# Folding the odd channels with mirrored token blocks in a Fourier filter beside a gated feed-forward

## The chip, the cores and the metric

One core of one Trainium2 chip. The metric is the device time of one execution in microseconds; lower is better. A core has TensorE (matmuls, PE in the profile), VectorE (DVE), ScalarE (ACT), GpSimd (POOL) and SyncE (SP, which here only issues transfers), each with an instruction stream of its own, and 16 DMA engines that move data.

## The reference

`x` is 2048 tokens of 512 channels in bfloat16. It is normalized over its channels, goes through two branches, and the three are added:

```
xn = (x - mean(x)) / sqrt(var(x) + 1e-5)                 # per token
A  = irfft2( rfft2(xn) * (w_r + 1j*w_i) )                # over tokens and channels; w is 2048 x 257
B  = ( gelu(xn @ w_gate) * (xn @ w_up) ) @ w_down        # 512 -> 1792 -> 512
out = x + A + B
```

## The kernel before

**The gated branch.** The tokens stand in 16 blocks of 128, four blocks (512 tokens) to a group. For each group and each of 14 chunks of 128 hidden columns, `gated` runs four matmuls with `wg` and four with `wu` (line 686) over the turned tokens `xnT`; ScalarE takes gelu of the one (691) and a copy of the other (692) out of PSUM, and VectorE multiplies them into `hT` (693). `down` (731) then makes one block of 512 output channels out of 14 matmuls, and the result is added to `x_sb` (740, or 742 for the last group). The first two token blocks go through `first` (705) block by block, so that TensorE can begin before the other two are normalized.

**The Fourier branch.** Line by line:

- Each block is normalized into `xn` (a part of `specB`) and turned so that channels stand on partitions: the first four blocks by TensorE (`turn`, 554, and a copy by VectorE, 559), the other twelve by a transposing DMA (`turn_dma`, 563).
- `fold` (577 to 586) adds and subtracts the four channel quarters of a turned group. Even channel frequencies need quarter 0 + 2 and 1 + 3, added and subtracted once more, and are left with 128 rows each. Odd ones need 0 - 2 and 1 - 3: two sets of 128 rows. Then each block is added to, and subtracted from, its own token mirror image.
- The channel transform (597) has a folded token block as weights and the cosines and sines in `smallc` as the moving side. For one block it runs four matmuls: two of 128 columns for the even frequencies, and two of 256 columns for the odd ones, which accumulate the two sets. One tile holds two blocks; there are eight tiles, and ScalarE copies each out (602).
- VectorE folds the tokens in three butterfly stages (783 to 811); eight matmul tiles `v` with the table `tokf` (820, 823) finish the token transform.
- The product with the filter `filt` and its mirror image (849 to 880) is VectorE's, in two halves `B` of four tiles `v`. The filter's mirrored half stands in other rows of `w_r` and `w_i`, in reversed order. It is written reversed into a DRAM scratch tensor `w_mirror` (657 to 659) and loaded from there (662 to 666).
- The way back is the same in reverse: matmuls with `toki` (900, 901), butterflies (916 to 944), matmuls with `smallc` (960), the last folds (969 to 972), and the sum with `x_sb` (974).

So that mirror images of token blocks fit, the blocks before are shifted by 64 tokens: block n holds tokens 128n - 64 to 128n + 64, and the one that wraps around is loaded and stored in two halves (`halves`). `SL` gives the order of the blocks.

**The order of the work.** A planner (`_Sched.run`) simulates all engines with a cost for each operation and writes a fixed order for each engine; the chip then keeps that order and waits on semaphores. The operation that can start first is taken, and keys break ties. The gated and down matmuls carry the largest keys in the order in which they are written, so TensorE does them whenever nothing else is ready: they are the filler. An operation of TensorE that becomes ready late is planned a `MARGIN` of 1 us later still. Normalization and statistics of blocks 4 to 15 have due times (`NORM`, `STAT`).

**The first loads.** ScalarE issues the first third of `smallc` (the identity among it) and the first 384 columns of `wg` and `wu`. SyncE issues all other loads in the order of their keys: the first blocks of `x` one by one, columns 384 to 768 of the weights, `x` blocks 4 to 7, columns 768 to 1280 and 1280 to 1792, the rest of `smallc`, `x` blocks 8 to 15. The list `gate` holds back: from the third load on, everything on SyncE waits until the first block of `x` has landed, and the later tables wait for given normalizations. Eight warm-up matmuls on zeros (`warm`, 511) run before the data arrives, and two more between the first turns.

Of the kernel before, what the change touches and what calls it, by code (L numbers as in the profile page):

```python
# [12 lines left out]
S = 2048  # L13
D = 512
# [21 lines left out]

def _constants():
# [4 lines left out]
    K[0] = 8 * (2 * (m % 64) + m // 64)  # L42
    for v, c in enumerate((4, 1, 9, 2, 10, 3, 11)):
        K[v + 1] = c + 16 * m
# [4 lines left out]
    si2[:, 0, 0] = np.sin(th * q * 1024)  # L49
    cof = co.copy()  # L50
    cof[:, 0, 0] *= 0.5
    low = (m < 64)[None]
    tf = []
    for a in (cof, si2):
        for part in (low, ~low):
            e = a[:64, 0] * part
            tf.append(np.concatenate([e, 0 * e] if a is cof else [0 * e, e]))
    for v, c in enumerate((4, 1, 9, 2, 10, 3, 11)):
        g = -1.0 if c > 8 else 1.0
        c = min(c, 16 - c)  # L60
        if c % 2:
            r = np.sin(np.pi * c / 2)
            f = r * g, r
        else:
            f = (-1.0, 1.0) if c == 4 else (g, -1.0)
        tf.append(np.concatenate([co[:64, v + 1], f[0] * si[:64, v + 1]]))
        tf.append(np.concatenate([g * co[:64, v + 1], f[1] * si[:64, v + 1]]))
    tf = np.stack(tf, 1)
    ci, sv = co[:64].transpose(2, 1, 0), si2[:64].transpose(2, 1, 0)
    sg = np.array([0, 1, 1, 1, 1, -1, -1, -1])[:, None]  # L70
# [3 lines left out]
    for a in (pr, pi):  # L74
        half = a[:, 0, 0:64].copy()
        a[:, 0] = np.concatenate([half * lo, half * ~lo], 1)
# [25 lines left out]
class _V:  # L102


    def __init__(self, ap, buf, idx, cell, part=(0, 1)):
        self.ap, self.buf, self.idx, self.cell, self.part = ap, buf, idx, cell, part

    def __getitem__(self, sl):
# [3 lines left out]
        part = tuple(h for h in self.part if lo < 64 * (h + 1) and hi > 64 * h)  # L112
# [238 lines left out]
def bass_parallel_sum__spectral_gfnet__glu_gated_geglu__prompt_kernel(  # L351
# [15 lines left out]
    SL = (1, 2, 3, 0) + tuple(range(4, 16))  # L367
    xb = A_x[0][64:S - 64].rearrange("(a q) d -> q a d", q=P)

    def halves(t, n):  # L370
        return [(slice(0, P), t[0][P * n - 64:P * n + 64])] if n else [(slice(0, 64), t[0][S - 64:S]), (slice(64, P), t[0][0:64])]

# [7 lines left out]
    with ExitStack() as es:  # L380
# [22 lines left out]
        small = sb("smallc", [11, P])  # L403
# [23 lines left out]
        Tf = small[:, 1:7]  # L427
        Ti = small[:, 7:11]
# [46 lines left out]


# [7 lines left out]
        first_row = None  # L484
        for s in range(4):
            for part, rows in halves(A_x, SL[s]):
                o = load("sp", x[part, s], rows, 1024 * (part.stop - part.start), key=next(k))
            first_row = o if s == 0 else first_row
# [3 lines left out]
        wload("act", wg, wgv, 0, 384, key=0.5)  # L492
        wload("act", wu, wuv, 0, 384, key=0.5)
        for w, v in ((wg, wgv), (wu, wuv)):
            wload("sp", w, v, 384, 768, key=next(k))
        load("sp", x[:, 4:8], xb[:, 3:7, :], 524288, key=next(k))
        for lo, hi in ((768, 1280), (1280, FF)):
            for w, v in ((wg, wgv), (wu, wuv)):
                wload("sp", w, v, lo, hi, key=next(k))
        load("sp", small[:, 2:11].rs([9 * P]), c_small.ap()[:, 2 * P:], 294912, key=next(k))  # L500
        for b in (2, 3):
            load("sp", x[:, 4 * b:4 * b + 4], xb[:, 4 * b - 1:4 * b + 3, :], 524288, key=next(k))
        op("pool", 0.1, lambda e: e.memset(eps.ap, LN_EPS), writes=(eps,), key=-2)
        op("pool", 0.1, lambda e: e.memset(half.ap, -0.5), writes=(half,), key=0)
        op("dve", 0.2, lambda e: e.memset(zero.ap, 0.0), writes=(zero,), key=-90)


        wt = _T("dn")

# [502 lines left out]
```

## Time and profile before

| what | value |
|---|---|
| median of 3 runs | 174.16 us (173.99 to 174.22) |
| the profiled execution's own time | 173.99 us |
| its span, first to last instruction | 172.2 us |
| TensorE busy | 167.9 us (98%) |
| VectorE busy | 143.3 us (83%) |
| ScalarE busy | 106.2 us (62%) |
| GpSimd busy | 11.8 us (7%) |
| moved by DMA | 16.35 MB |

How to read it: a row of a group names the line, the engine, the operation, what it writes and reads, the shapes, how often (x), then the busy time in us and the mean of one in ns, and at last the idle time of the engine ahead of it with what ended that. Matmuls are pipelined and their ends are modelled, so the time of one is longer than the distance from one to the next. A line can be a helper's: 472 is every tensor-tensor operation of the Fourier branch, 468 every plain load. In the rows of transfers the number is the time from issue to landing. `SPq` and `ACTq` are the issuing of transfers. PEld is the loading of weights into TensorE.

### The profile page before, as it was taken

To read this page: it belongs to the slowest core of one execution; us is meant where nothing else is said; L and a number is where in the kernel's file an instruction comes from. 1 tells how busy PE (TensorE), PEld (TensorE's weight loads), DVE (VectorE), ACT (ScalarE), POOL (GpSimd) and SP (SyncE) were. 2 spreads that over 40 slices of the span, in tenths; PEclk is the share of its full clock that TensorE was granted. 3 is DMA by queue.
4 is the path that set the end of the run, shared out by engine and by line. 5 is a ranking of instruction groups with operands and counts; after the bars stand their busy time and mean duration, and the time that the engine had idled before them with its cause. 6 is when DMAs were issued, how large, how long until landed. Compare 5 with 4: busy or idle time off the path is not lost.

```text
span 172.2 us, 2683 instructions
## 1 busy us (share of the span) xinstructions
PE 167.9 (98%) x994; PEld 87.1 (51%) x994; DVE 143.3 (83%) x283; ACT 106.2 (62%) x172; POOL 11.8 (7%) x25
## 2 busy tenths in 40 slices
PE   7899999999999999999999999999999999999994
PEld 2588544455574444444444464554445664444443
DVE  2779899998539999967999999979999949972931
ACT  3378666675894647969645495794636996562000
POOL 2222234300000000030000000000000000000000
PEclk9999999999999999999999999999999999999999
DMA  5999999967532224920000000000000002410311
GB/s 150 299 356 354 298 145 300 231 151 144 122 81 63 61 52 97 308 71 4 0 2 0 0 4 0 0 0 0 4 0 2 0 4 81 129 36 0 122 64 61
DMA packets 24333, 16.35 MB, mean 95 GB/s; under 512 B 7679, under 2 KB 23936, under 8 KB 24320
## 3 DMA queue, kind: packets, MB, share of 16 engines
q1 hardware_dynamic: 23120, 15.32, 35.3%
q10 hardware_dynamic: 1200, 0.85, 1.6%
q8 instruction: 8, 0.13, 0.3%
q14 instruction: 5, 0.04, 0.1%
HBM read 12.50 MB, written 3.15 MB: 91 GB/s over the span
## 4 chain that ended last, share of the span: by engine, by line
PE 93%; DMA 4%; ACT 1%; DVE 1%; issue 0%; DVEq 0%
PE ps_gu L686 55%; PE ps_dn L731 21%; PE ps_sp L731 7%; DMA x_sb<-in_A_x_dram 4%; PE ps_sp L597 3%; PE ps_sp L960 2%; PE ps_sp L820 2%; PE ps_sp L900 1%; PE ps_sp L901 1%; ACT gg L716 1%; PE ps_sp L823 1%; DVE bst L524 0%; PE ps_gu L705 0%; PE ps_sp L554 0%; ACT uu L717 0%
## 5 line engine op out<-in xcount | busy, mean ns | idle before, releaser
L686 PE MATMUL ps_gu<-xnT,wu 128*128 128x512 bf16 (+1 forms) x236 | 56.7, 363 | 0.2 <-ACT gg L716 0.2
L686 PE MATMUL ps_gu<-xnT,wg 128*128 128x512 bf16 (+1 forms) x236 | 56.7, 363 | 0.0
L691 ACT ACTIVATE gg<-ps_gu 128x512 bf16<-128x512 f32 (+1 forms) x59 | 33.6, 570 | 13.1 <-PE ps_gu L686 10.4
L692 ACT ACTIVATE uu<-ps_gu 128x512 bf16<-128x512 f32 (+1 forms) x59 | 33.7, 572 | 10.8 <-PE ps_gu L686 10.5
L731 PE MATMUL ps_dn<-wd,hT 128*128 128x512 bf16 x168 | 38.9, 379 | 0.0
L686 PEld LDWEIGHTS ps_gu<-xnT,wg 128*128 128x128 bf16 x236 | 22.8, 98 | 22.9 <-DVE xnT L559 0.3
L686 PEld LDWEIGHTS ps_gu<-xnT,wu 128*128 128x128 bf16 x236 | 22.7, 98 | 22.9 <-ACT gg L716 0.4
L472 DVE TENSOR_TENSOR specB<-specB 128x1024 bf16<-128x1024 bf16 (+2 forms) x47 | 29.3, 662 | 1.5 <-ACT specB L965 1.4
L731 PEld LDWEIGHTS ps_dn<-wd,hT 128*128 128x128 bf16 x168 | 16.4, 98 | 19.1
L693 DVE TENSOR_TENSOR hT<-gg,uu 128x512 bf16<-128x512 bf16 (+1 forms) x59 | 22.5, 396 | 3.1 <-ACT uu L692 3.1
L739 ACT ACTIVATE db<-ps_dn 128x512 bf16<-128x512 f32 x12 | 7.2, 597 | 18.6 <-PE ps_dn L731 18.5
L524 DVE BATCH_NORM_STATS2 bst<-x_sb 128x6 f32<-128x512 bf16 x16 | 10.9, 685 | 3.6 <-DMA x_sb<-in_A_x_dram 3.6
L472 DVE TENSOR_TENSOR specC<-specB 128x1024 bf16<-128x1024 bf16 (+5 forms) x21 | 12.8, 634 | 0.2
L731 PE MATMUL ps_sp<-wd,hT 128*128 128x512 bf16 (+2 forms) x70 | 12.3, 336 | 0.0
L472 DVE TENSOR_TENSOR specB<-specA 128x2048 bf16<-128x2048 bf16 x8 | 9.4, 1220 | 2.9 <-ACT specA L602 2.4
L740 DVE TENSOR_TENSOR x_sb<-db,x_sb 128x512 bf16<-128x512 bf16 x12 | 5.0, 417 | 6.7 <-ACT db L739 6.7
L731 PEld LDWEIGHTS ps_sp<-wd,hT 128*128 128x128 bf16 x70 | 6.3, 97 | 6.1 <-DVE x_sb L742 0.2
L472 DVE TENSOR_TENSOR specB<-specB,filt 128x2048 bf16<-128x2048 bf16 x8 | 9.4, 1216 | 0.0
L828 ACT ACTIVATE specA<-ps_sp 128x1024 bf16<-128x1024 f32 x8 | 8.0, 1024 | 1.6 <-PE ps_sp L820 1.3
L602 ACT ACTIVATE specA<-ps_sp 128x1024 bf16<-128x1024 f32 x8 | 7.8, 1028 | 1.7 <-PE ps_sp L597 1.6
L965 ACT ACTIVATE specB<-ps_sp 128x1024 bf16<-128x1024 f32 x8 | 7.8, 1031 | 0.4 <-PE ps_sp L960 0.4
L906 ACT ACTIVATE specC<-ps_sp 128x1024 bf16<-128x1024 f32 x8 | 7.8, 1039 | 0.0
(64 smaller groups left out, 131.2 us busy)
## 6 DMA issues: line engine op xcount, KB each, us to landing
wd<-in_B_w_down_dram SPq DMA_DIRECT2D x1, 1792.0 KB, 8.8
out_dram<-x_sb SPq DMA_DIRECT2D x14, 128.0 KB, 1.8
x_sb<-in_A_x_dram SPq DMA_DIRECT2D x3, 512.0 KB, 8.8
wg<-in_B_w_gate_dram SPq DMA_DIRECT2D x2, 512.0 KB, 7.5
wu<-in_B_w_up_dram SPq DMA_DIRECT2D x2, 512.0 KB, 8.2
filt<-w_mirror SPq DMA_DIRECT2D x6, 128.5 KB, 5.2
toki<-c_ti SPq DMA_DIRECT2D x1, 768.0 KB, 7.9
tokf<-c_tf SPq DMA_DIRECT2D x1, 576.0 KB, 4.3
```

What stands on the lines that cost most here:

```text
L472: return op("dve", c_tt(n), lambda e: e.tensor_tensor(o.ap, a.ap, b.ap, f), reads=(a, b), writes=(o,), key=key, **kw)
L524: op("dve", 0.61, lambda e: e.bn_stats(bst[:, s].ap, xs(s).ap), reads=(xs(s),), writes=(bst[:, s],), key=key, due=due, after=after)
L602: op("act", c_act(1024), lambda e, yv=yv, t=t: e.activation(yv.ap, spair(t).rearrange("p (s r i) -> p s i r", s=4, r=4), ACT.Copy), writes ...
L686: ins = e.matmul(gub(t, n), w.ap[:, dc, fc * P:(fc + 1) * P], xnT.ap[:, b, sl, dc, :], start=(dc == 0), stop=(dc == 3))
L691: op("act", c_act(n), lambda e: e.activation(gg.ap[:, gs.slot, 0:n], gub(g, n), ACT.Gelu_apprx_tanh), tiles=(g, gs), key=0.0)
L692: op("act", c_act(n), lambda e: e.activation(uu.ap[:, us.slot, 0:n], gub(u, n), ACT.Copy), tiles=(u, us), key=0.0)
L693: op("dve", c_tt(n), lambda e: e.tensor_tensor(hT.ap[:, h.slot, lo:lo + n], gg.ap[:, gs.slot, 0:n], uu.ap[:, us.slot, 0:n], MUL), tiles=(g ...
L731: ins = e.matmul(bank(), hT.ap[:, hs[(b, fc)].slot, sl * P:(sl + 1) * P], wd.ap[:, fc, lo:lo + n], start=(fc == 0), stop=(fc == NFC - 1))
L739: op("act", c_act(n), lambda e: e.activation(db.ap[:, d.slot, 0:n], bank(), ACT.Copy), tiles=(t, d), key=0.0)
L828: op("act", c_act(1024), lambda e, xv=xv, t=t: e.activation(xv.ap, spair(t), ACT.Copy), writes=(xv,), tiles=(t,), key=-0.5)
L906: op("act", c_act(1024), lambda e, gv=gv, t=t: e.activation(gv.ap, spair(t).rearrange("p (k x i) -> p k x i", k=4, x=4), ACT.Copy), writes ...
L965: op("act", c_act(1024), lambda e, rv=rv, t=t: e.activation(rv.ap, spair(t), ACT.Copy), writes=(rv,), tiles=(t,), key=-0.5)
```

## The change

- The token blocks are the plain ones, tokens 128n to 128n + 127; `halves` and `SL` go, and each block is one load and one store.
- The odd channels are folded once more, as the even ones are. For that the second pair's difference is needed with its channels reversed: a new function `mirror` takes quarter 1 minus quarter 3 of the normalized block, read backwards along the channels, and turns it by itself, for the first group on TensorE and for the other three by a transposing DMA. `fold` then adds it to and subtracts it from quarter 0 minus quarter 2. The channel matrices shrink from six to four blocks of 128 columns, and the two matmuls of 256 columns become two of 128.
- The rows of the token tables (`tokf`, `toki`, the frequencies on partitions) run backwards in blocks of 32. With this the mirrored filter comes directly from `w_r` and `w_i`, and the near one is loaded reversed within blocks of 32; the DRAM scratch goes. The filter loads wait for the last mirrored difference. The rows for frequency zero move from partition 0 to partition 96.
- The last butterfly of the first token tile (a sum and a difference) goes into the table `tokf`.
- The order of the tiles `v` in the token transform and back changes, and the halves `B` take every second tile.
- The start: the first block is normalized, turned and copied in two halves (`first_half`); the reciprocal root for the second block is ScalarE's and VectorE's, not GpSimd's; the loads on SyncE wait, from the third on, for the third warm-up matmul and not for the first block; `x` blocks 8 to 11 go ahead of the last weight columns; the first token block's matmuls do all of `wg` ahead of `wu`, and the first of them waits for half of the channels.

The diff, cut to its core:

```diff
@@ the constants
-    for d0, r in ((0, (0,)), (0, (2,)), (0, (1, 3)), (P, (1, 3))):
-        kk = np.concatenate([np.arange(i, 256, 4) for i in r])[None]
-        ks = np.where(kk == 0, 256, kk)
-        a = 2.0 * np.pi / D * (d0 + np.arange(P) + 0.5)[:, None]
-        fwd += [np.cos(a * kk), np.sin(a * ks)]
+    a = 2.0 * np.pi / D * (np.arange(P) + 0.5)[:, None]
+    for r in (0, 2):
+        kk = np.arange(r, 256, 4)[None]
+        fwd += [np.cos(a * kk), np.sin(a * np.where(kk == 0, 256, kk))]
+    odd = np.concatenate([np.arange(1, 256, 4), np.arange(3, 256, 4)])[None]
+    fwd += [np.cos(a * odd), np.sin(a * odd)]
...
@@ the first loads
-            if s == 1:
-                gate.append(first_row)
...
+        rows(0, 1)
+        rows(1, 2)
+        gate.append(warms[2])
+        for i in (2, 3):
+            rows(i, i + 1)
         for w, v in ((wg, wgv), (wu, wuv)):
             wload("sp", w, v, 384, 768, key=next(k))
...
+        rows(4, 8)
+        for w, v in ((wg, wgv), (wu, wuv)):
+            wload("sp", w, v, 768, 1280, key=next(k))
+        rows(8, 12)
+        for w, v in ((wg, wgv), (wu, wuv)):
+            wload("sp", w, v, 1280, FF, key=next(k))
+        load("sp", small[:, 2:9].rs([7 * P]), c_small.ap()[:, 2 * P:], 229376, key=next(k))
+        rows(12, 16)
...
@@ the first block
+        def first_half(h):
+            cs = slice(2 * h, 2 * h + 2)
+            i, r, o = xs(0)[:, 256 * h:256 * h + 256], xn(0)[:, cs].rs([256]), xnT[:, 0, 0, cs].rs([256])
...
+            op("dve", 0.2, lambda e: e.tensor_scalar(r.ap, i.ap, bag.ap[:, 0, 0:1], rs.ap[:, 0:1], SUB, MUL), ...)
+            op("pe", 2 * 0.107, f, reads=(r, ident), tiles=(t,), key=-70.0, lag=0.1)
+            op("dve", 0.21, lambda e: e.tensor_copy(o.ap, bank()), writes=(o,), tiles=(t,), key=-70.0)
...
@@ the mirrored difference, and fold
+        def mirror(b):
+            rows = RB(8192 + 2048 * (b % 2), [4, 4, P])
+            g = RB(2048 * (b % 2) + 1024, [4, P])
+            odd[b] = RB(2048 * (b % 2) + 1536, [4, P])
+            tt(g, rows[:, :, 1, ::-1], rows[:, :, 3, ::-1], SUB, 512, 0.5)
+            if b:
+                op("sp", 1.25, lambda e: e.dma_start_transpose(odd[b].ap, g.rs([512]).ap), ..., dma=425000, key=-5.0)
+                return
...
+            op("pe", 4 * 0.056, f, reads=(g, ident), tiles=(t,), key=2.0, lag=0.1)
+            op("dve", 0.34, lambda e: e.tensor_copy(odd[b].rs([512]).ap, bank()), ..., key=1.0)
...
-            tt(f[:, :, 2:4], xt[:, :, 0:2], xt[:, :, 2:4], SUB, 1024, kk)
-            for i, n in ((0, 3), (3, 1)) if b == 0 else ((0, 4),):
...
+            tt(f[:, :, 3], xt[:, :, 0], xt[:, :, 2], SUB, 512, kk)
+            tt(f[:, :, 2], f[:, :, 3], odd[b], SUB, 512, kk)
+            tt(f[:, :, 3], f[:, :, 3], odd[b], ADD, 512, kk)
...
-                            to = bank[:, :, 2 * cc] if cc < 2 else bank[:, :, 1::2]
-                            mat = Tf.ap[:, cc] if cc < 2 else Tf.ap[:, 2 * cc - 2:2 * cc]
-                            ins = e.matmul(to, z.ap[:, p + o, cc, :], mat, start=(cc == 0), stop=(cc == 3))
+                            to = bank[:, :, 2 * cc] if cc < 2 else bank[:, cc - 2, 1::2]
+                            ins = e.matmul(to, z.ap[:, p + o, cc, :], Tf.ap[:, cc], start=(cc == 0), stop=(cc == 3))
...
@@ the filter
+        gate.append(hold[16])
         for ri, src in ((0, A_w_r), (1, A_w_i)):
...
+            near = src.rearrange("(a b c) k -> a b (c k)", a=4, b=32)[:, ::-1, 257:8 * 257]
+            far = src.rearrange("(a b c) k -> a b c k", a=4, b=32)
+            load("sp", W[:, ri, 0, 1:8], near, 460544, key=next(k), cost=0.55)
+            for h in range(4):
+                load("sp", W[32 * h:32 * h + 32, ri, 1, 1:8], far[3 - h, :, 15:8:-1], 115136, key=next(k), cost=0.55)
...
@@ the token transform
-        u = Fb[:, 2:4]
-        tt(u, s2[:, 0:2], s2[:, 2:4], ADD, 1024)
-        tt(H[:, 14], u[:, 0], u[:, 1], ADD, 512)
-        tt(H[:, 15], u[:, 0], u[:, 1], SUB, 512)
+        tt(H[:, 14:16], s2[:, 0:2], s2[:, 2:4], ADD, 1024)
...
-        for v, hh in enumerate(((14, 15), (12, 13), (0, 1), (4, 6), (8, 9), (10, 11), (2, 7), (5, 3))):
+        for v, hh in ((4, (12, 13)), (0, (14, 15)), (2, (8, 9)), (6, (10, 11)), (1, (0, 1)), (7, (4, 6)), (3, (2, 7)), (5, (5, 3))):
...
```

More of the change, by code (lines that the diff above doesn't have):

```diff
@@ L111, in __getitem__ @@
         lo, hi, _ = sl[0].indices(P)
-        part = tuple(h for h in self.part if lo < 64 * (h + 1) and hi > 64 * h)
+        part = tuple(h for h in self.part if lo < 32 * (h + 1) and hi > 32 * h)
         return _V(self.ap[sl], self.buf, self.idx[sl[1:]], self.cell, part)
@@ L474, in bass_parallel_sum__spectral_gfnet__glu_gated_geglu__prompt_kernel, with warm @@
         ADD, SUB, MUL = ALU.add, ALU.subtract, ALU.mult
+        op("dve", 0.2, lambda e: e.memset(zero.ap, 0.0), writes=(zero,), key=-90)
+        wt = _T("dn")
+        def warm(key):
+            return op("pe", 0.427, lambda e: e.matmul(ps_dn[:, :], zero.ap[:, 0:P], zero.ap, start=True, stop=True), reads=(zero,), tiles=(wt,), key=key)
+        warms = [warm(-50) for _ in range(WARM)]
         def load(q, dst, src, nbytes, **kw):
@@ L631, in bass_parallel_sum__spectral_gfnet__glu_gated_geglu__prompt_kernel @@
             if s % 4 == 3:
+                mirror(s // 4)
+                hold[16] = sch.ops[-2]
                 fold(s // 4)
```

190 lines of the change are left out of this document (88 added, 102 removed).

## The prediction

> **What bounds the kernel now.** I read the page first (busy times, the chain that ended last), then the waits of TensorE, then the chain in order of time.
>
> ```profile
> span 172.2 us, 2683 instructions
> ...
> PE 167.9 (98%) x994; PEld 87.1 (51%) x994; DVE 143.3 (83%) x283; ACT 106.2 (62%) x172; POOL 11.8 (7%) x25
> ...
> PE 93%; DMA 4%; ACT 1%; DVE 1%; issue 0%; DVEq 0%
> ```
>
> TensorE is busy 98% of the span, and 93% of the chain that ended last is its own work. Its waits (us in total, times, longest) are three:
>
> ```profile
> PE ps_dn L511 <- DVE zero L505: 1.2, 1, 1.2
> PE ps_gu L705 <- DVE xnT L559: 0.5, 1, 0.5
> PE ps_gu L686 <- ACT gg L716: 0.2, 1, 0.2
> ```
>
> L511 is the warm-up on zeros; the other two lie in the first 11 us, as the rows of part 2 show. So two things move the end: what is taken from or added to TensorE's work, and when its unbroken run begins. All else counts only where it makes TensorE wait. The chain (start us, us, what) gives the pieces:
>
> ```profile
> 11.55 0.45 PE ps_sp L554 x8
> ...
> 36.94 1.32 PE ps_sp L597 x16
> ...
> 133.06 0.89 PE ps_sp L960 x16
> ...
> 157.80 12.14 PE ps_sp L731 x70
> 169.96 0.29 DVE x_sb L742
> ```
>
> **Part 1: the channel matmuls (L597), on TensorE's path.** A tile of two token blocks has eight matmuls, four of 128 columns and four of 256; there are eight tiles (64 matmuls in all). Two tiles (x16) take 1.32 us, so 0.66 each. After the change all eight have 128 columns, since the odd channels come folded and there is no second half to accumulate. L960 has that very form, a token block as weights and 128 columns of smallc moving, and its x16 take 0.89 us: 0.445 a tile. Eight tiles save 8 x (0.66 - 0.445) = 1.72 us. The other end of the bound is that the weight loads set the pace, as there stays one for each matmul:
>
> ```profile
> L731 PEld LDWEIGHTS ps_dn<-wd,hT 128*128 128x128 bf16 x168 | 16.4, 98 | 19.1
> ```
>
> A load of 128 x 128 lasts 98 ns. Eight of them in series are 0.78 us a tile, 8 x 0.12 = 1.0 us more than now in all. I take 0.445, as the L960 row has one load to each matmul and still runs at 0.89 / 16 = 56 ns: the loads overlap. The Trainium skill (TensorE: Matmul & The Clock Gate, "Back-to-back issue gap") speaks against this change: it says that a stream of pairs of load and matmul sustains about 81 ns at 128 columns, and that 56 ns under-counts. By that a tile would be an estimated 0.65 us and the eight tiles would save 0.1 us. The L960 row, 56 ns in such a stream, disagrees.
>
> Block 0's mirrored half is turned on TensorE by four matmuls like those of L554, 0.45 / 8 x 4 = 0.23 us more. All other matmuls keep their number and shape: the token stage's first tile (four matmuls), the inverse stages, the gated and the down matmuls. Part 1: -1.72 + 0.23 = **-1.5 us**.
>
> **Part 2: the start.** Rows picked from the merged order of time (start us, us, engine, line):
>
> ```profile
> 1.17 4.45 PE L511 MATMUL ps_dn<-zero 128*128 128x512 bf16 x10 [1.17 <-DVE zero L505]
> ...
> 3.25 0.69 DVE L524 BATCH_NORM_STATS2 bst<-x_sb 128x6 f32<-128x512 bf16 x1 [2.14 <-DMA x_sb<-in_A_x_dram]
> ...
> 5.46 0.44 PE L554 MATMUL ps_sp<-smallc,specB 128*128 128x128 bf16 x4
> 5.50 0.51 SPq L468 DMA_DIRECT2D wu<-in_B_w_up_dram  x1
> ...
> 6.42 0.40 PE L705 MATMUL ps_gu<-xnT,wg 128*128 128x128 bf16 x4 [0.52 <-DVE xnT L559]
> ...
> 7.34 0.69 DVE L524 BATCH_NORM_STATS2 bst<-x_sb 128x6 f32<-128x512 bf16 x1 [0.65 <-DMA x_sb<-in_A_x_dram]
> ...
> 7.91 0.39 PE L705 MATMUL ps_dn<-xnT,wu 128*128 128x128 bf16 x4
> ...
> 8.42 0.40 PE L705 MATMUL ps_gu<-xnT,wg 128*128 128x128 bf16 x4
> ...
> 9.77 0.60 PE L686 MATMUL ps_gu<-xnT,wg 128*128 128x256 bf16 x4
> ...
> 10.52 0.60 PE L686 MATMUL ps_gu<-xnT,wu 128*128 128x256 bf16 x4 [0.15 <-ACT gg L716]
> ...
> 11.92 0.69 DVE L524 BATCH_NORM_STATS2 bst<-x_sb 128x6 f32<-128x512 bf16 x1 [0.33 <-DMA x_sb<-in_A_x_dram]
> ...
> 12.71 0.60 PE L686 MATMUL ps_gu<-xnT,wu 128*128 128x256 bf16 x4
> 13.32 0.61 PE L686 MATMUL ps_gu<-xnT,wg 128*128 128x256 bf16 x4
> ```
>
> At 56 ns a 128-column matmul and 112 ns a 256-column one (so a group issues in 0.23 or 0.45 us, shorter than the printed times, which hold the last one's end), TensorE's issue has four gaps: 5.69 to 6.42 (0.73), 8.14 to 8.42 (0.28), 10.22 to 10.52 (0.30), 13.16 to 13.32 (0.16). Together 1.47 us: the most that a better start can give.
>
> The first gap is the copy of the turned block 0, done in one piece. The change normalizes, turns and copies it in halves, and the first group's first two matmuls need only the first half. The warm-up (L511, ten at 0.44) still holds TensorE up to 5.46, so I put the first L705 near 6.0. The second gap: VectorE took the statistics of the third block of x ahead of the copy that TensorE needed, and waited until 7.34 for that block's load. The fourth is the same once more, behind statistics that waited until 11.92 for the next load. For the third, the transfers (KB, us to landing) say more than the releaser named:
>
> ```profile
> wu<-in_B_w_up_dram SPq DMA_DIRECT2D x1, 384.0 KB, 4.9
> ```
>
> wu's second piece, issued at 5.50, lands at 10.4, and TensorE goes on at 10.52. So three gaps of four hang on how early SyncE issues. Before, its third load waits until the first block of x has landed (3.25). After, it waits for the third warm-up matmul, 1.17 + 3 x 0.44 = 2.5, and one load less (the wrapped block's two halves) stands ahead of the weights. That is 0.75 us earlier, and for the weights up to 0.5 more (the issue at 5.50 lasts 0.51). The transfers can use only part of it, as the windows show (DMA share and GB/s last):
>
> ```profile
> 5.50:6.00 0.50, 0.40 (x5) 0.23 (x4) 0.06 (x1) 0.49 (x2) 0.42 (x1) 1.00 1.10 375
> 6.00:6.50 0.50, 0.07 (x2) 0.08 (x3) 0.50 (x2) 0.01 (x1) 0.16 (x1) 1.00 1.10 254
> 6.50:7.00 0.50, 0.50 (x8) 0.37 (x9) 0.19 (x1) 0.00 (x0) 0.00 (x0) 1.00 0.55 87
> 7.00:7.50 0.50, 0.50 (x13) 0.50 (x11) 0.16 (x1) 0.00 (x0) 0.00 (x0) 1.00 0.79 253
> ```
>
> From 6.0 to 7.5 the engines moved (121 + 288 + 122) x 0.5 = 266 KB less than at 375 GB/s, which is 0.7 us of transfer: the hole that the late issue left. Filling it brings every later load 0.7 us forward at most. Against it: the first pieces of wg and wu, issued by ScalarE, share the engines with what SyncE now issues sooner. I take 0.6 us of the 1.47; the bounds are +0.3 (wu's first piece pushed back by one x block, 128 KB at 375 GB/s) and -1.47. Part 2: **-0.6 us**.
>
> **Part 3: VectorE, off the path.**
>
> ```profile
> L472 DVE TENSOR_TENSOR specB<-specB 128x512 bf16<-128x512 bf16 x16 | 6.1, 416 | 0.0
> ...
> L472 DVE TENSOR_TENSOR specB<-xnT 128x1024 bf16<-128x1024 bf16 x8 | 5.2, 680 | 0.0
> ```
>
> Each block's fold loses one operation of 1024 and gains four of 512 (the mirrored difference, the first pair's difference, and their sum and difference): 4 x 0.416 - 0.68 = +1.0 us, +4.0 for four blocks. The token stage loses one of 1024 and two of 512 and gains one of 1024, -0.8. The copy of block 0's turned half is +0.4 and the joining of its two split folds about -0.3. Net +3.3 us, nothing on the path as long as gelu products and the spectral result come in time (rival B).
>
> **Part 4: the queue of SyncE.** Three more turns by DMA stand in it, each behind its block's other four, and the filter loads behind the last mirrored difference.
>
> ```profile
> L563 SPq DMA_TRANSPOSE xnT<-specB x12: 1188/1280/2376, 16.9 to 37.4; - x12
> ...
> DMA to landing us min/median/max: 3.2/4.2/7.1
> ...
> 38.73 4.36 SPq L468 DMA_DIRECT2D filt<-in_A_w_r_dram  x7
> ...
> 48.55 6.20 SPq L468 DMA_DIRECT2D w_mirror<-in_A_w_r_dram  x3
> ...
> 81.25 4.64 DVE L472 TENSOR_TENSOR specB<-specB,filt 128x2048 bf16<-128x2048 bf16 x4
> ```
>
> A turn is issued in 1.3 us and lands after 4.2, at worst 7.1. The filter is first read at 81.25. Reversing 1024 rows through DRAM took 6.2 us of issue, 6 ns a row; the direct loads move about 1300 rows for each part, so 2 x 7.8 us, and begun near 40 (the direct loads of before begin at 38.73, just behind the turns) they are issued by about 60. Cost nothing, with some 15 us in hand after a landing like that of a turn; without that cover VectorE would stall by what is lacking.
>
> **Sum.** On the profiled execution (173.99 us, of which 1.8 lie outside the span): -1.5 - 0.6 = -2.1, 171.9. The median of the runs shown is 174.16, 0.17 above it: **172.0 us**, likely 171.3 to 172.6.
>
> **Rivals.** A: the start gives nothing. wu's first piece lands later because x and the second pieces share the engines, and the gaps move but stay: 0 to +0.3 in place of -0.6, hence 172.6 to 173.0. For it: 375 GB/s at 5.5, no room there. Against it: the hole after 6.5.
>
> B, slower: the spectral result comes late to the last block. TensorE still has the last L731 run at 157.80, and VectorE must by then have added the spectral rows.
>
> ```profile
> 133.00:158.00 25.00, 25.00 (x165) 13.19 (x163) 19.06 (x35) 17.32 (x26) 0.00 (x0) 1.00 0.14 43
> ```
>
> VectorE (third busy time) has 5.9 us free there; TensorE's shorter run takes 1.5 of them. So a lateness above 4.4 us decides. VectorE's 3.3 us, and a last turn that lands in 7.1 rather than 4.2 (2.9) behind an issue of its own 1.3 us, make 7.5: 3.1 us too many, 175.1. Against it: the fold runs where VectorE has time between waits, and the early part of the spectral work has other slack. C: weight loads pace L597: +1.0 + 0.23 - 0.6, 174.8; at 81 ns a matmul -0.1 + 0.23 - 0.6, 173.7. Against it the L960 row. D: the planner's new order loses as much as the work saves (a wait of 2 us anywhere in TensorE's run): 174.1; nothing in the rows speaks for a place.
>
> **How the numbers follow.** Forecast 0.60; A 0.17; C at 81 ns 0.03, C at 98 ns 0.02; B 0.13; D 0.05. About 0.2% (0.35 us) is what this kernel's measurement can tell from no change. Faster is forecast, A and C at 81 ns: 0.80, less 0.02 for a start that loses more; same is D, 0.05; slower is B, C at 98 ns and that rest, 0.17. Range: from all four gaps closed (174.16 - 1.5 - 1.47 = 171.2, and 0.1 for the scatter of the runs: 171.1) up through A and C at 81 ns to D, 174.2.
>
> **What would show it.** Right: L597 has 64 matmuls of 128 columns at about 0.445 us a tile in the chain; TensorE's busy time falls by about the 1.5; the first L705 is near 6.0 and the wait before the first wu group of L686 is gone; VectorE busy near 146.6; no wait of TensorE after 14 us. Wrong: x16 of L597 above 1.2 us (C); a wait of L597 on specC, or of the last L731 on x_sb (B); the first L686 again near 9.8 and a hole in the DMA share (A).

## The result, and the profile after

The changed kernel takes 172.06 us (median of 4 runs, 171.99 to 172.15), the kernel before 174.07 us beside it (4 runs, 173.87 to 174.22). The ratio is 0.9885, with a 95% interval of 0.9868 to 0.9902: 1.7 to 2.3 us faster. The forecast was 172.0. The profiled execution after took 172.02 us, its span 170.0; the span is 2.2 us shorter.

First, from the page of the kernel after, the busy times and the chain by engine.

```profile
PE 166.2 (98%) x998; PEld 85.9 (51%) x998; DVE 146.1 (86%) x295; ACT 106.0 (62%) x173; POOL 11.5 (7%) x23
...
PE 95%; DMA 3%; DVE 1%; issue 0%; DVEq 0%
```

TensorE's busy time fell by 1.7 us, VectorE's rose by 2.8, and TensorE's share of the chain went from 93 to 95%. TensorE bounds the kernel as before, with less work. The waits of TensorE after (us in total, times, longest) are down to one, the warm-up on zeros:

```profile
PE ps_dn L476 <- DVE zero L470: 1.2, 1, 1.2
```

The two other waits of before, 0.5 and 0.2 us, are gone from this view, and there is none later than 14 us. The groups by form and the chain (start us, us, what) show the channel matmuls, which were L597 and are now L631:

```profile
L631 PE MATMUL ps_sp<-smallc,specC 128*128 128x128 bf16 x64 | 4.4, 219 | 0.0
...
42.03 0.89 PE ps_sp L631 x16
...
64.62 0.43 PE ps_sp L851 x2
...
98.29 0.06 PE ps_sp L931
...
130.83 0.89 PE ps_sp L991 x16
...
155.57 12.14 PE ps_sp L766 x70
```

All 64 have 128 columns now. Sixteen take 0.89 us where they took 1.32, which is 56 ns a matmul. (The 219 ns of the group is one matmul from start to end; the next is issued before that.) The same places in the chain of the kernel before that were not shown above:

```profile
61.24 0.43 PE ps_sp L820 x2
...
98.79 0.06 PE ps_sp L900
```

Read against each other, these rows tell where the spectral part ran late. The channel matmuls begin 5.1 us later than before (42.03 to 36.94), the token transform 3.4 later (64.62 to 61.24), the next spectral step 0.5 earlier (98.29 to 98.79), the inverse channel step 2.2 earlier (130.83 to 133.06), and the last run 2.2 earlier (155.57 to 157.80). The extra work on VectorE did delay the spectral part by several us, as rival B feared. By 98 us it had been made up with no wait of TensorE, since the gated matmuls filled its time.

The start, from the timeline of TensorE after (start us, us, engine, line):

```profile
5.44 0.54 PE L567 MATMUL ps_sp<-smallc,specB 128*128 128x128 bf16 x4
6.11 0.77 PE L737 MATMUL ps_gu<-xnT,wg 128*128 128x128 bf16 x8
...
7.61 0.39 PE L737 MATMUL ps_dn<-xnT,wu 128*128 128x128 bf16 x4
8.09 0.40 PE L737 MATMUL ps_gu<-xnT,wg 128*128 128x128 bf16 x4
...
9.44 0.60 PE L718 MATMUL ps_gu<-xnT,wg 128*128 128x256 bf16 x4
9.92 0.60 PE L718 MATMUL ps_gu<-xnT,wu 128*128 128x256 bf16 x4
10.43 0.61 PE L718 MATMUL ps_gu<-xnT,wg 128*128 128x256 bf16 x4
...
12.89 0.60 PE L718 MATMUL ps_gu<-xnT,wg 128*128 128x256 bf16 x4
```

With the issue times of the prediction (0.23 us for four matmuls of 128 columns, 0.45 for four of 256), the gaps are now 5.67 to 6.11 (0.44, was 0.73), 7.84 to 8.09 (0.25, was 0.28), 9.89 to 9.92 and 10.37 to 10.43 (0.09, was 0.30); the fourth (0.16) is gone. That is 0.78 us in place of 1.47. (The prediction's list left out a fifth gap: four matmuls issue in 0.23, and in before the next L705 after the one at 6.42 begins at 6.79, 0.14 too late. After has about as much between the halves, in the x8 row that lasts 0.77 where a later one of its form lasts 0.61, so the difference stands.) The seventh group of 256 columns begins at 12.89 rather than 13.32, although block 0's mirrored turn (four matmuls, 0.23) now stands ahead of it: 0.43 + 0.23 = 0.66 us won by the start. The sum closes: 1.72 - 0.23 + 0.66 = 2.15 against 2.2 in the span. It is a sum over one pair of profiles; the start scatters by several tenths, as said under Part 2.

### The profile page after: what moved, and what is told of

Its sections match the earlier page's. It is cut to its first block, busy times and chain, and to the rows that moved or that the text cites. A ratio compares the mean times of both kernels' runs of the same rounds, so it can differ in the third digit from the quotient of the medians.

```text
span 170.0 us, 2695 instructions
## 1 busy us (share of the span) xinstructions
PE 166.2 (98%) x998; PEld 85.9 (51%) x998; DVE 146.1 (86%) x295; ACT 106.0 (62%) x173; POOL 11.5 (7%) x23
## 4 chain that ended last, share of the span: by engine, by line
PE 95%; DMA 3%; DVE 1%; issue 0%; DVEq 0%
PE ps_gu L718 55%; PE ps_dn L766 21%; PE ps_sp L766 7%; DMA x_sb<-in_A_x_dram 3%; PE ps_sp L631 2%; PE ps_sp L991 2%; PE ps_sp L851 2%; PE ps_sp L931 1%; PE ps_sp L932 1%; PE ps_dn L476 1%; PE ps_gu L737 1%; PE ps_sp L854 1%; DVE bst L520 0%; PE ps_dn L737 0%; PE ps_sp L550 0%; DVE xnT L555 0%
## 5 line engine op out<-in xcount | busy, mean ns | idle before, releaser
L718 PE MATMUL ps_gu<-xnT,wg 128*128 128x512 bf16 (+1 forms) x236 | 56.7, 363 | 0.0
L718 PE MATMUL ps_gu<-xnT,wu 128*128 128x512 bf16 (+1 forms) x236 | 56.7, 363 | 0.0
L466 DVE TENSOR_TENSOR specB<-specB 128x512 bf16<-128x512 bf16 (+2 forms) x58 | 33.1, 609 | 3.8 <-DMA specB<-specB 2.3
L718 PEld LDWEIGHTS ps_gu<-xnT,wu 128*128 128x128 bf16 x236 | 22.8, 98 | 23.2
L718 PEld LDWEIGHTS ps_gu<-xnT,wg 128*128 128x128 bf16 x236 | 22.6, 98 | 22.3 <-ACT uu L752 0.2
L725 DVE TENSOR_TENSOR hT<-gg,uu 128x512 bf16<-128x512 bf16 (+1 forms) x59 | 22.6, 393 | 1.7 <-ACT uu L724 1.6
L466 DVE TENSOR_TENSOR specC<-specB 128x1024 bf16<-128x1024 bf16 (+2 forms) x18 | 12.4, 712 | 0.2
```

Source lines behind the costliest of these rows:

```text
L466: return op("dve", c_tt(n), lambda e: e.tensor_tensor(o.ap, a.ap, b.ap, f), reads=(a, b), writes=(o,), key=key, **kw)
L718: ins = e.matmul(gub(t, n), w.ap[:, dc, fc * P:(fc + 1) * P], xnT.ap[:, b, sl, dc, :], start=(dc == 0), stop=(dc == 3))
L725: op("dve", c_tt(n), lambda e: e.tensor_tensor(hT.ap[:, h.slot, lo:lo + n], gg.ap[:, gs.slot, 0:n], uu.ap[:, us.slot, 0:n], MUL), tiles=(g ...
```

## The experiments

Every kernel here was run beside the kernel before, so ratios are to that; after's is 0.9885. The planner writes each engine's order afresh for each kernel. b_gate keeps before's order on every engine, a_gate0 keeps after's, and a_ord0 keeps after's on all but SyncE. For the others the order moved elsewhere too, which is said where it matters.

### The shorter matmuls

a_rep: the changed kernel with the first quarter of each token block's contraction issued three times (the two added ones are overwritten), so that TensorE again streams as many columns as in before.

```
+  for _ in range(2 if cc == 0 else 0):
+      e.matmul(to, z.ap[:, p + o, cc, :], Tf.ap[:, cc], start=True, stop=True)
   ins = e.matmul(to, z.ap[:, p + o, cc, :], Tf.ap[:, cc], start=(cc == 0), stop=(cc == 3))
```

> The changed kernel with two more matmuls of 128 columns for each token block in the channel transform (the first matmul of each block is issued three times, the repeats are overwritten), so that the columns streamed are again those of before, 768 a block. Theory (56 ns a matmul, all of it on TensorE's path): 16 x 2 x 0.056 = 1.8 us slower than the changed kernel, 173.8 to 173.9. Rival 1 (weight loads set the pace at 98 ns): 3.1 us slower, 175.2. Rival 2 (the channel matmuls are not what ends last): less than 0.5 us slower.

Measured: 173.87 us, ratio 0.9988 (0.9968 to 1.0008), span 171.8. Against after the median rises by 1.81 and the span by 1.8. In the chain of a_rep one token block's six matmuls (two added, four of old) read:

```profile
41.99 0.11 PE ps_sp L632 x2
42.10 0.22 PE ps_sp L633 x4
```

0.33 us for six is 56 ns each, and 32 added ones make 1.8. TensorE has no wait but the warm-up's here either, so the added time is the matmuls' own. It follows that a matmul of 128 columns costs its 56 ns on the path, and that Part 1 is the bulk of the gain. With before's columns restored, what is left of the gain is 0.4 us by the medians and the spans and 0.2 by the ratio, whose interval includes none at all; 0.66 - 0.23 of the start and the mirrored turn would be 0.43.

### The start, part by part

b_gate: the kernel before, with SyncE's third load held behind the third warm-up matmul instead of behind the first block of x. Nothing else.

```
-  gate.append(first_row)
+  gate.append(warms[2])
```

> The kernel before, with one thing of the change: from the third load on, SyncE waits for the third warm-up matmul, not for the first block of x. Theory (three of the four gaps at the start hang on how early SyncE issues): 0.3 to 0.5 us faster than before, about 173.6 to 173.8; wu's second piece lands near 9.4 to 9.9 and the first wu group of L686 starts some 0.1 us behind it, in place of 10.52. Rival 1 (the first block's halves give the start's gain, the gate nothing): no change, within 0.1 us. Rival 2 (that third gap is ScalarE's reading of the PSUM bank, as the profile names it): the group still waits for ScalarE and starts no more than 0.1 us earlier than ScalarE's own shift.

Measured: 174.08 us, ratio 1.0004 (0.9976 to 1.0032), span 172.4. The 0.3 to 0.5 us that were expected did not come: the earlier gate alone is worth nothing that shows. wu's second piece is issued at 4.91 rather than 5.50, but the chain, the waits of TensorE and the timeline of b_gate say that it lands later than before, and that the first turn is late too:

```profile
4.91 5.67 DMA wu<-in_B_w_up_dram
...
PE ps_sp L554 <- DVE specB L541: 0.6, 1, 0.6
...
PE ps_gu L686 <- DMA wu<-in_B_w_up_dram: 0.3, 1, 0.3
...
10.71 0.60 PE L686 MATMUL ps_gu<-xnT,wu 128*128 128x256 bf16 x4 [0.27 <-DMA wu<-in_B_w_up_dram]
```

4.91 + 5.67 = 10.58, against 10.40. The first turn (L554) begins at 5.83 rather than 5.46, as VectorE waited 0.40 us for the second block of x and the first block's normalization stands behind its statistics. So in this profile an earlier third load went with a later second one. Two things follow. The third gap is the landing of wu, as the prediction read it: here the releaser itself is the DMA. And an earlier issue doesn't bring the landing forward by itself.

a_gate0: the changed kernel with the gate put back behind the first block of x.

```
-  rows(0, 1)
+  gate0 = rows(0, 1)
   rows(1, 2)
-  gate.append(warms[2])
+  gate.append(gate0)
```

> The changed kernel with the gate of before: from the third load on SyncE waits for the landing of the first block of x. Theory (the gate moves the landing of wu's second piece and of the third x block only a little, as in the kernel of before, where the gate alone gave nothing): 0 to 0.3 us slower than the changed kernel, 172.1 to 172.4. Rival (the prediction's account, gate worth most of the start): 0.4 to 0.7 slower.

Measured: 172.31 us, ratio 0.9892 (0.9875 to 0.991), span 170.4. The median is 0.25 us above after's, and the intervals overlap. wu's second piece is issued at 4.62 rather than 3.99, TensorE waits 0.4 us before the first wu group, and at the seventh group it is still 0.38 behind (13.27 for 12.89). So the gate is worth 0 to 0.4 us, not the 0.75 by which it opens earlier.

a_copy1: the statistics of the third and fourth block both put behind the copy of block 1, to close the second gap.

```
-  if s == 0:
-      stats(2, -30.0, None, (sch.ops[-2],))
-  stats(3, -30.0, None, (sch.ops[-2],))
+  copy1 = sch.ops[-2]
+  for s in (2, 3):
+      stats(s, -30.0, None, (copy1,))
```

> The changed kernel with the statistics of block 2 behind the copy of block 1 on VectorE, so that TensorE's second gap (7.84 to 8.09) no longer waits for the third load of x. Theory (that gap is the statistics' wait for the load): the gap closes and the kernel is 0.15 to 0.3 us faster than the changed one, 171.8 to 171.9. Rival (blocks 2 and 3 then come later and TensorE waits for them instead): same or up to 0.3 us slower.

Measured: 172.22 us, ratio 0.9892 (0.9874 to 0.991), span 170.8: no gain. The second gap is gone, and the first wu group comes later than in after:

```profile
wu<-in_B_w_up_dram SPq DMA_DIRECT2D x1, 384.0 KB, 6.7
...
10.83 0.60 PE L718 MATMUL ps_gu<-xnT,wu 128*128 128x256 bf16 x4 [0.67 <-ACT gg L723]
```

Issued at 3.99 and 6.7 us to landing is 10.7. The view names ScalarE's gg as the releaser, as it did for the third gap of before; the landing at 10.7 is what fits a start at 10.83. Here a gap closed ahead of a transfer only moved the wait to the transfer. (After's piece, issued at the same 3.99, landed in 5.8 us, at 9.8. This profile fell on a late landing, and its wait of 0.67 is not the price of the edit; that nothing was gained is what the medians say.)

a_whole: the changed kernel with the first block of tokens normalized, turned and copied in one piece, as in before (and the old order of its first groups).

```
-  root_act(1, 1, -58.0)
-  for h in range(2):
-      first_half(h)
+  root_pool(1, 1, -50.0)
...
-  norm(s, -60.0)      # for s > 0 only
-  turn(s, 1, -60.0)
+  norm(s, -60.0)      # for every s
+  turn(s, 1, -60.0)
```

> The changed kernel with the first block normalized, turned and copied in one piece, the second block's root on GpSimd, and wg and wu in turn in the first block's matmuls, as before. Theory: the first L705-like matmul starts 0.3 to 0.4 us later, near 6.4 to 6.6, but the next gap, the copy of block 1, takes most of it up: 0.1 to 0.3 us slower than the changed kernel, 172.15 to 172.35. Rival (the halves are the start's gain): 0.5 us slower or more.

Measured: 173.21 us, ratio 0.9939 (0.992 to 0.9959), span 171.4: 1.15 us above after's median, well over what was expected. The waits of TensorE in a_whole besides the warm-up:

```profile
PE ps_gu L734 <- DVE xnT L555: 0.5, 1, 0.5
PE ps_gu L715 <- ACT gg L720: 0.4, 1, 0.4
PE ps_sp L631 <- DVE specC L466: 0.4, 1, 0.4
```

The first is the gap of before, back in its place: the first L734 begins at 6.74, the first L737 of after at 6.11. The two others lie later and come with the rewritten order. By the seventh group, 0.21 us are lost (13.10 against 12.89). So the halves, with the second block's root and the first order that went with them, carry about a third of the 0.66 in this profile. The 0.4 us at 21.50 and the 0.4 at 51.69 are most of the rest; what the halves alone are worth is not separated.

### The order of the loads

a_ord0: the changed kernel with the load of x blocks 8 to 11 put back behind the last columns of the weights and the small constants.

```
-  rows(8, 12)
   for w, v in ((wg, wgv), (wu, wuv)):
       wload("sp", w, v, 1280, FF, key=next(k))
   load("sp", small[:, 2:9].rs([7 * P]), c_small.ap()[:, 2 * P:], 229376, key=next(k))
+  rows(8, 12)
```

> The changed kernel with x blocks 8 to 11 loaded behind the last weight columns and the rest of smallc, as before; nothing else. Theory after the first four runs (the kernel with the old start lost 1.2 us where VectorE, at 20.35, stood before the statistics of block 8 and TensorE had to wait for gelu products behind it): the stall comes back, 0.8 to 1.5 us slower than the changed kernel, 172.9 to 173.6, with a wait of TensorE on ScalarE between 18 and 24 us. Rival (that stall came from other parts of the old start): within 0.2 us of the changed kernel, 172.06.

Measured: 173.56 us, ratio 0.9961 (0.9947 to 0.9976), span 171.4. This one move is worth 1.5 us by the medians, 1.3 by the ratios and 1.4 by the spans, with every other engine's order unchanged. The waits, the chain and the timeline of a_ord0 show how:

```profile
PE ps_gu L718 <- ACT gg L723: 1.2, 2, 0.9
...
11.35 9.12 DMA x_sb<-in_A_x_dram
...
20.50 0.69 DVE L520 BATCH_NORM_STATS2 bst<-x_sb 128x6 f32<-128x512 bf16 x1 [1.61 <-DMA x_sb<-in_A_x_dram]
...
22.13 0.60 ACT L723 ACTIVATE gg<-ps_gu 128x512 bf16<-128x512 f32 x1 [1.61 <-DVE hT L725]
...
22.78 1.04 PE L718 MATMUL ps_gu<-xnT,wu 128*128 128x512 bf16 x4 [0.31 <-ACT gg L723]
```

It is a row of three engines behind a transfer: VectorE stands 1.61 us at the statistics of block 8, whose load was issued at 11.35 and landed at 20.5. The gated product (L725, at 21.81) is queued behind those statistics, ScalarE's next gelu waits 1.61 us for the buffer that this product frees, and TensorE waits for the bank that ScalarE frees. At 22.78 that costs 0.31 us. The larger part of TensorE's 1.2 us comes later, 0.89 at 35.93: VectorE, which in after is busy for all 16.70 us from 13.3 to 30, makes up nothing. At 34.83 it is still 1.6 us behind after (33.25) with the product that ScalarE's next gelu waits for. In after the load is issued at 7.33 and VectorE comes to it without a wait; in before it was issued behind the weights too, and VectorE came later and waited 0.44:

```profile
18.94 0.68 DVE L520 BATCH_NORM_STATS2 bst<-x_sb 128x6 f32<-128x512 bf16 x1
```
```profile
20.87 0.69 DVE L524 BATCH_NORM_STATS2 bst<-x_sb 128x6 f32<-128x512 bf16 x1 [0.44 <-DMA x_sb<-in_A_x_dram]
```

(The upper row is after's timeline, the lower one before's.) So the move is a cover: it adds nothing to the gain of the matmuls and the start, but without it 1.3 to 1.5 us of that gain are given back.

b_ord: the same move in the kernel before.

```
   for w, v in ((wg, wgv), (wu, wuv)):
       wload("sp", w, v, 768, 1280, key=next(k))
+  xl(2)
   for w, v in ((wg, wgv), (wu, wuv)):
       wload("sp", w, v, 1280, FF, key=next(k))
   load("sp", small[:, 2:11].rs([9 * P]), ...)
-  for b in (2, 3): ...
+  xl(3)
```

> The kernel before with x blocks 8 to 11 loaded ahead of the last weight columns; nothing else. Theory (that load binds only where TensorE runs earlier and VectorE has the mirrored folds as well: the trace of before has 0.44 us of waiting for it on VectorE and none on TensorE): same as before, within 0.2 us. Rival (the load order is a gain by itself, 1.5 us as in the changed kernel): 172.6 to 173.2.

Measured: 174.16 us, ratio 0.9994 (0.9971 to 1.0016), span 172.8. That is no change. The profiled execution was 0.45 us slower than the median, with a new wait of TensorE:

```profile
PE ps_gu L690 <- DVE xnT L563: 1.1, 1, 1.1
```

Up to there no engine's order of lines but SyncE's differs from before's (VectorE's does from 19.8 us on). The copy (L563) stands behind the statistics of block 4, whose load landed at 12.5; in before they begin at 11.92. The load was issued at the same time in both (6.04 and 6.05), so either the move of the other load delays it or the landing scatters by that much. What the move would be worth in before without that wait can't be told from this run: inconclusive.

a_start0: the changed kernel with all of the start undone at once: the gate, the load of x blocks 8 to 11, the halves and the old first order.

```
-  gate.append(warms[2])
+  gate.append(gate0)
...
+  rows(8, 12)          # behind the weights and the constants
...
-  first_half(h)        # as in a_whole
```

> The changed kernel with the start of before: gate on the landing of the first block, first block normalized, turned and copied in one piece, root of the second block on GpSimd, the old order of the first matmuls and of the loads of x blocks 8 to 11. Theory: about 0.65 us slower than the changed kernel (1.5 faster than before), 172.6 to 172.8. Rival (the new blocks and matmuls bring it all): as the changed kernel, 172.0 to 172.1.

Measured: 174.32 us, ratio 1.0003 (0.9974 to 1.0032), span 172.2: all of the gain is gone, where a loss of 0.65 us was expected, although the channel matmuls are still the short ones. Read alone it would say that the start is everything. Its waits say otherwise:

```profile
PE ps_gu L715 <- ACT gg L720: 1.2, 1, 1.2
PE ps_gu L734 <- DVE xnT L555: 0.5, 1, 0.5
PE ps_sp L631 <- DVE specC L466: 0.4, 1, 0.4
```

The first row is the stall of a_ord0 again (block 8's statistics wait 1.27 us at 20.35), the second the gap that a_whole reopened, and the third is a wait of the channel matmuls on the fold. By its seventh group a_start0 has lost only 0.26 us to after (13.15 against 12.89); the greater part goes behind 20 us. The start is thus an enabler here more than a sum of its gaps.

b_start: the kernel before with all of the start of the change, the halves, the gate and the loads, and none of the rest.

```
-  gate.append(first_row)
+  gate.append(warms[2])
...
+  first_half(h)        # block 0 in halves, as in after
+  xl(2)                # x blocks 8 to 11 ahead of columns 1280 and up
```

> The kernel before with the whole start of the change (gate on the third warm-up matmul, first block in halves, second block's root on ScalarE, wg ahead of wu in the first block's matmuls, x blocks 8 to 11 ahead of the last weight columns), but its own shifted blocks, channel matmuls and filter path. Theory (the gain is the sum of about 0.65 us at the start and 1.5 us of TensorE's work, each by itself): 0.65 us faster than before, about 173.4. Rival (the start only helps because later work is shorter, or the gain is all in the matmuls): within 0.2 us of before.

Measured: 176.75 us, ratio 1.013 (1.0098 to 1.0162), span 174.1: 2.3 us slower than before by the ratio, 1.9 by the spans, where 0.65 us faster was expected. The first 13 us are won as in after, though by less (its seventh group begins at 13.15 rather than 13.32). Later the rewritten order loses:

```profile
PE ps_sp L618 <- DVE specC L472: 1.1, 1, 1.1
PE ps_sp L758 <- DVE x_sb L769: 0.7, 1, 0.7
...
49.45 1.29 DVE L472 TENSOR_TENSOR specB<-xnT 128x1024 bf16<-128x1024 bf16 x2 [3.41 <-DMA xnT<-specB]
```

VectorE waits 3.41 us for a turn by DMA, the channel matmuls wait 1.1 for the fold behind it, and the last run waits 0.7 for the spectral rows. Together 1.8 us, about what the spans differ by. SyncE's rows show where the turn was: it is issued at 46.95, behind filter loads that begin at 38.39, where before issues its last two turns from 36.15 and only then the filter, from 38.73. The changed kernel holds the filter loads for the last mirrored difference, and b_start does not. This is rival D's case, an order that loses 2 us, and it came with a part of the change, not with the whole.

### The rivals' places

a_pemir: all mirrored halves turned on TensorE, none by DMA.

```
-  if b:
+  if b > 3:
...
-  hold[16] = sch.ops[-2]      # the filter loads still wait for the last mirrored difference
+  hold[16] = sch.ops[-3]
```

> The changed kernel with the mirrored differences of all four groups turned by TensorE and copied by VectorE, in place of three transposing DMAs. That takes away VectorE's longest wait of the middle (2.3 us for such a DMA) and adds 12 turns of 0.056 us. Theory (only TensorE's work counts, VectorE's wait was hidden): 0.7 us slower than the changed kernel, 172.7 to 172.9. Rival B of the prediction (the lateness of the spectral part is paid): 172.0 or faster, up to 1.5 us.

Measured: 172.69 us, ratio 0.9897 (0.9869 to 0.9925), span 170.9. In after VectorE waits 2.25 us for the third of these turns. The timeline of VectorE, and SyncE's own row:

```profile
49.78 0.88 DVE L466 TENSOR_TENSOR specB<-specB 128x512 bf16<-128x512 bf16 x2 [2.25 <-DMA specB<-specB]
...
41.81 1.25 SPq L592 DMA_TRANSPOSE specB<-specB  x1
```

In a_pemir that wait is gone, and the time is no better: the median is 0.63 above after's and the span 0.9. Three blocks' turns are 3 x 0.23 = 0.7 of TensorE, and by the seventh group, ahead of any difference between the two kernels, this execution is already 0.25 behind after's (13.14 for 12.89): together the 0.9. The intervals of the two ratios overlap, so the size isn't shown. No time came back with the late turns gone, and in after TensorE has no wait there: they cost nothing.

a_late4 and a_late8: one addition of 2048 elements in the token stage issued four or eight times more, so that VectorE is late by that much.

```
-  tt(s2, Fb[:, 0:4], Fb[:, 4:8], ADD, 2048)
+  for _ in range(1 + 4):
+      tt(s2, Fb[:, 0:4], Fb[:, 4:8], ADD, 2048)
```

> The changed kernel with one 2048-element sum of the token butterfly issued four times more, 4 x 1.14 = 4.6 us of VectorE's work on the chain of the spectral part. Theory (VectorE has 5.7 us free between 133 and 158 us, which the spectral part can use before the last down matmuls need its rows): at most 0.5 us slower than the changed kernel, 172.1 to 172.6. Rival B's point of 4.4 us, taken from the changed kernel on: the same here. If lateness is paid at once: 176.6.

> As the run with four repeats, with eight: 9.1 us of VectorE's work more. Theory: beyond the slack of about 5.7 us the rest is paid at the end, 9.1 - 5.7 = 3.4 us: 175 to 176. If VectorE can hide more, by work that it does between its other waits: 172.5 to 174. If all is paid: 181.

An operation of this size takes 1.15 us a piece in a row of them (the timeline row under Part 4 has four in 4.62), so 4.6 and 9.2 us were added. Measured: 172.94 (ratio 0.9916, 0.9886 to 0.9947) and 178.88 (1.0255, 1.022 to 1.0291), 0.3 and 2.9 us above what was expected. The waits of TensorE, of a_late4 and then of a_late8:

```profile
PE ps_sp L766 <- DVE x_sb L777: 0.7, 1, 0.7
```
```profile
PE ps_sp L766 <- DVE x_sb L777: 4.9, 1, 4.9
```

The last run waits on the spectral rows, in the very place that rival B named. 4.6 - 0.7 = 3.9 and 9.2 - 4.9 = 4.3: the changed kernel has about 4 us to spare there, not the 5.7 of the expectations.

The medians rise by 0.9 and 6.8 us, more than the waits. For a_late8 the granted clock of its page, in 40 slices, and its chain show the rest:

```profile
PEclk9999999999999999999999999999999999999879
...
166.69 3.32 PE ps_sp L766 x8
```

After TensorE had stood still for 4.9 us, its granted clock was 0.50 from about 166.2 to 169.6, and eight matmuls of 512 columns took 3.32 us, 0.42 each, where they are 0.22 apart in after. The 41 matmuls that were left took 7.67 us for after's 6.03. 4.9 + 1.6 = 6.5, of 6.6 by which the span is longer. In a_late4, whose wait was 0.7, the clock stayed at 1.00; there 0.3 us more went in a wait for ScalarE's gelu at 35.05, which came with the rewritten order, and 0.4 of the 1.4 by the spans isn't accounted for.

## Why the prediction was right, and where its steps were not

**Part 1 was right, for the reason given.** -1.72 for the matmuls and +0.23 for the mirrored turn stood in the sum. L631 has 64 matmuls, 0.445 us a tile in the chain, and a_rep puts the price of 32 of them at 1.81 us. Rival C is out: at 81 ns a matmul x16 would have been 1.30 us, and it is 0.89. The rule of the Trainium skill (TensorE: Matmul & The Clock Gate, "Back-to-back issue gap") would have put the time at an estimated 173.7; the trace's 56 ns disagrees with it for this stream.

**Part 2 had the right size, 0.66 for 0.6, on an account that was wrong in half; that the size fits is in part luck.** The first L737 came at 6.11 (said: near 6.0), the hole in the transfers was filled (below), and the third gap was wu's landing. But the step "three gaps of four hang on how early SyncE issues" failed. b_gate made SyncE earlier and gained nothing; a_gate0 made it later and lost 0.25 by the medians, within the intervals. The second gap hung on that issue by the prediction's words and hardly moved (0.28 to 0.25), since VectorE still took the statistics first and the load still came after them; with a_gate0's later issue it was smaller (7.94 to 8.01):

```profile
7.01 0.69 DVE L520 BATCH_NORM_STATS2 bst<-x_sb 128x6 f32<-128x512 bf16 x1 [0.38 <-DMA x_sb<-in_A_x_dram]
```

In eight kernels wu's second piece was issued at 3.99, and it landed between 9.4 (a_rep) and 10.7 (a_copy1), in the middle of them 9.7; in before and b_ord, with the issue at 5.50 and 5.49, at 10.4 and 9.9. So 1.5 us earlier at the queue were worth some 0.4 at the landing, with a scatter of as much. The start as a whole scatters too: five more kernels with after's start (a_rep, a_ord0, a_pemir, a_late4, a_late8) reach the seventh group between 12.75 and 13.14, and b_ord, with before's orders there, has no second gap and reaches the sixth at 12.24, where before has 12.71. So the 0.66 of one pair of profiles is not known better than to some tenths. How the rest of the 0.66 splits among the block without two partial loads, the halves and the earlier gate is open: the parts taken one at a time do not add up.

**What the prediction left out.** It named the move of x blocks 8 to 11 nowhere, though it is in the list of the change. The move holds 1.3 to 1.5 us, more than half of the gain. By the same working a change without it would have been forecast at 172.0 and measured at 173.6; that the total came out is in this respect luck. The row that could have told stood in the trace of before: block 8's statistics waited 0.44 us at 20.87 already, so any change that brings VectorE there earlier needs that load earlier too.

**Part 3 was right.** VectorE's busy time is 146.1 (said: near 146.6), and it is hidden, though with nothing to spare from 13.3 to 30 us (see a_ord0). Its free time in the last stage (third busy time) is hardly less than before's, 25.00 - 19.29 = 5.7 us for 5.9:

```profile
133.00:158.00 25.00, 25.00 (x154) 12.65 (x151) 19.29 (x36) 15.62 (x24) 0.00 (x0) 1.00 0.13 43
```

**Part 4 was right that it is free, wrong on the landing.** The third turn, issued at 41.81, was awaited until 49.78: 8.0 us, over the 7.1 taken as the worst, and the median of the three is 6.2, not 4.2. It stood among the filter loads on SyncE's queue, two of them ahead of it and the others behind. The filter was first read at 81.60, and its main loads had been issued by 62:

```profile
specB<-specB SPq DMA_TRANSPOSE x3, 6.2
...
81.60 4.62 DVE L466 TENSOR_TENSOR specB<-specB,filt 128x2048 bf16<-128x2048 bf16 x4
```

**Rival B** was weighed rightly. Its place and its point are confirmed (about 4 us measured, 4.4 said); the lateness it feared came, 5.1 us at the channel matmuls, and was made up by 98 us, as the argument against it had it ("other slack"). **Rival A** is out, as L718 begins at 9.44 and not near 9.8. **Rival D** did not come with the whole change, but b_start and a_whole show that a planner's order can lose 1 to 2 us when only a part is made or undone.

## What to carry to other kernels

Work taken from the engine that bounds a kernel is priced well by the spacing of rows of the very same shape in the chain, not by their durations. Putting off a load that the bounding engine doesn't wait for still has a price: look at which engine reads it first, and what is queued behind that read. Where an order is planned anew for each version, take a part of the change for its price only if the other engines' orders stayed the same, else read the waits before the time.

## What the runs showed of the hardware

The transfers of the queues in the stretch from 3.4 to 5.4 us (packets, MB, share of 16 engines; q10 carries ScalarE's loads, q1 SyncE's), in before and then in after:

```profile
q10 hardware_dynamic: 861, 0.65, 101.7%
q1 hardware_dynamic: 9, 0.01, 0.9%
```
```profile
q10 hardware_dynamic: 881, 0.66, 102.5%
q1 hardware_dynamic: 20, 0.01, 2.5%
```

ScalarE's weights took all of the engines in both kernels. In after SyncE's third load had been issued at 2.67, 0.6 us earlier than before's (3.25), and its queue moved next to nothing until 5.4 all the same. Whether the queues don't share here, or that load wasn't ready to move, the rows don't tell; either way it fits with how little an earlier gate bought. What did change is the stretch from 6.5 to 7.5, in before and then in after:

```profile
DMA packets 224, 0.17 MB, mean 170 GB/s; under 512 B 7, under 2 KB 224, under 8 KB 224
```
```profile
DMA packets 449, 0.34 MB, mean 340 GB/s; under 512 B 12, under 2 KB 449, under 8 KB 449
```

The hole is filled, 170 KB more, a half of a microsecond at 340 GB/s. A turn by DMA of 128 x 512 elements landed 8.0 us after its issue when it stood among loads of the filter, against a median of 4.2 for the turns of before.

A stop of TensorE of 4.9 us (a_late8) was followed by 3.4 us at a granted clock of 0.50, while stops of 0.7 us (a_late4) and 1.2 us (a_start0) left it at 1.00.
